# Linear attention, gated MLP and SoLU MLP on one core: where the small side products of a block and of the last layer stand in the engines' queues

## The chip, the cores and the metric

One NeuronCore of a Trainium2 chip. The metric is the device time of one execution in microseconds (us), as the median of several runs.

## The reference, cut to what matters

Eight batches of 576 tokens with 8 heads of 64 give 4,608 tokens of width 512.

```
q_s = softmax(q, over d);  k_s = softmax(k, over the sequence)
x   = q_s @ (k_s^T @ v)                      # per batch and head
y   = (silu(x @ w_gate) * (x @ w_val)) @ w_out            # d_ff 1536
h   = y @ w_in                                            # 512 -> 1024
s   = h * softmax(h);  out = (layernorm(s) * g_ln) @ w_out2
```

## The kernel before, in words

All matrix products are fp32 in three passes: each operand is split into a high part in fp32r and a low part (the rest), and `mm3` (L931 to L933) adds high x high, high x low and low x high. One pass is a matmul of 128x128 by 128x512.

The first layer runs in nine blocks of 512 tokens. A block has 12 slices of d_ff, and a slice takes three steps on PE, which the code calls gaps: `wg` (gate), the output product `y` of the slice two before it, and `wv` (value). So a block has 36 gaps of 12 matmuls. `block` sorts a table of tasks by gap; tasks of the same gap are recorded after the block's own step. The order of recording is the order in each engine's queue, and nothing reorders it later. `tasks_of(j)` puts the side work of block j there: the attention of the next tokens (gap 5: POOL's subtraction L540; gap 8: `q_max`, a DVE reduction and then POOL's subtraction L682; gap 9: `kv_exp`, the exp L601 on ACT; gap 11: `kv_mm`, the small product `pk` on PE, L610, that reads this exp; gap 14: `q_norm`, which ends in POOL's product L700; gaps 20, 24 and 26 the second half of k and v in the same way), and `y_forms_at`.

`y_forms_at` prepares y of the block before for the second layer. The product h = y w_in is done by seven products of halves instead of eight (Strassen's way in Winograd's form), for which y is needed in seven forms: three are quarters of y, four are sums and differences of them. `Y_FORMS` lists them in the order in which they are made: 0 to 2 plain, 3 to 6 with a sum. A form takes a sum on DVE (L895, only for forms 3 to 6), a cast on ACT (L913), the low part on DVE (L915), and two stores to DRAM (L917).

The second layer runs over 18 pairs of 128-token tiles. `emit_pair(p)` is the seven products (42 matmuls, named by their form: 1, 6, 5, 2, 7, 3, 4) with the additions that make h of them: `c` (ACT, L1342) copies the first product away before product 2 is accumulated on its bank. `emit_rest(p)` is the softmax, SoLU and the layer norm's sums of both tiles, their 16-bit halves `w`, the DMA transposes that turn them (`wT`), and the output products `emit_out` (48 matmuls) of the pair before. The turned halves are joined (`zt`, L1429 on DVE and L1432 on ACT) and split (`zhl`, L1440 on ACT, L1443 on DVE) inside the next pair's `emit_pair`. Its queue on ACT is, in this order: store, split of the first tile, `c`, join and split of the second tile.

The last block's y has no later block to make its forms in. Its last two output products run before pair 0's products and after them, `y_keep` copies y out of PSUM, and `y_make` makes the forms of pairs 16 and 17 in SBUF, seven in a row, in `emit_rest(14)` and `emit_rest(15)`. For the other pairs `y_load` brings the forms from DRAM.

Of the kernel before, what the change touches and what calls it, by code (L numbers as in the profile page):

```python
# [9 lines left out]
F32 = mybir.dt.float32  # L10
F32R = mybir.dt.float32r
# [5 lines left out]
PSUM = bass.MemoryType.PSUM  # L17
DRAM = bass.MemoryType.DRAM

P = 128  # L20
# [23 lines left out]
    banks=3,  # L44
# [161 lines left out]
def attention_glu_solu_kernel(  # L206
# [23 lines left out]
    nc = tc.nc  # L230
# [16 lines left out]
    NB = len(BLOCKS)  # L247
# [5 lines left out]
    def f32(ap):  # L253
        return ap.bitcast(F32)
# [21 lines left out]
    yf_dram = dram.tile([NT2 // 2, P, 2, 7, 2 * P], F32, name="yf_dram")  # L276
# [518 lines left out]
    tmp = ph1.enter_context(tc.tile_pool(name="tmp", bufs=1, reuse_waits="tile"))  # L795
# [8 lines left out]
    def at(t, g, f, *a):  # L804
        t.setdefault(g, []).append((f, a))
# [54 lines left out]
    ADD, SUB = ALU.add, ALU.subtract  # L860
    KH = KD // 2
    yts, yz = {}, {}

    def y_keep(j):


        if j < NB - 1:
            yt = tmp.tile([P, KD, Y2], F32, tag="yt", bufs=1, name="yt")
            halves_ = [yt[:, r * KH:(r + 1) * KH] for r in range(2)]
        else:  # L870
            halves_ = [apool.tile([P, KH, Y2], F32, tag="a", bufs=2, name="yt") for r in range(2)]
        for k in range(KD):
            o = halves_[k // KH][:, k % KH]
            if k % 2:
                nc.scalar.copy(out=o, in_=ys[j][k])
            else:
                nc.vector.tensor_copy(out=o, in_=ys[j][k])
        del ys[j]
        yts[j] = halves_

    def y_quarter(j, n, r):

        v = yts[j][r].rearrange("p k (q n t) -> p n q k t", q=2, n=2)
        return v[:, n]
# [34 lines left out]
    def y_forms_at(t, j):  # L919


        tasks = [Task(y_form, (j, n)) for n in range(7)]
        for n, g in enumerate((5, 6, 7, 8, 10, 12, 14)):
            at(t, g, tasks[n].step)
            at(t, g + 1, tasks[n].finish)

# [57 lines left out]
    def next_o(lag):  # L984
        if len(pend) > lag:
            emit_o(*pend.pop(0))
# [107 lines left out]
    psA = ExitStack()  # L1094
    w_b = wb.enter_context(tc.tile_pool(name="wb", bufs=1, reuse_waits="tile"))
    gv_pool = psA.enter_context(tc.tile_pool(name="ps_gv", bufs=4, space=PSUM))
# [130 lines left out]
    NP2 = NT2 // 2  # L1227
    FH = DF2 // 2
# [39 lines left out]

    yq = {}

    def q_tiles(p):
        homes = ((att, "qt"), (w_b, "b6")) if p % 2 else ((att, "kt"), (att, "vt"))
        yq[p] = [pool.tile([P, 7, KH, P], F32R, tag=tag, name=n) for (pool, tag), n in zip(homes, ("yh", "yl"))]

    def y_load(p):
        q_tiles(p)
        for n in range(2):
            nc.sync.dma_start(
                out=f32(yq[p][n]).rearrange("p i k t -> p (i k t)"),
                in_=yf_dram[p, :, n].rearrange("p i w -> p (i w)"),  # L1280
            )

    def y_make(p, n):

        j, q = divmod(p, 2)
        if n == 0:
            q_tiles(p)
        i, x, with_ = Y_FORMS[n]
        of = lambda n, r: y_quarter(j, n, r)[:, q]
        if with_:  # L1290
            if x and with_[0]:
                yz[j] = stat.tile([P, KH, P], F32, tag="m", bufs=1, name="yz")
            y_sum(yz[j], of, x, with_)
            s = yz[j]
        else:
            s = of(*x)
        yh, yl = (y[:, i] for y in yq[p])
        nc.scalar.copy(out=yh, in_=s)
        nc.vector.tensor_tensor(out=yl, in0=s, in1=f32(yh), op=SUB)

    t = tasks_of(NB - 1)
    at(t, 0, x_load)
# [9 lines left out]
    for p in range(2):  # L1312
        at(t, 28, y_load, p)
    block(NB - 1, range(NF), t)
    next_o(1)
    psA.close()
    l2s = ExitStack()
    ps_h = l2s.enter_context(tc.tile_pool(name="ps_h", bufs=1, space=PSUM, reuse_waits="tile"))

    ctx.enter_context(tc.manual_schedule())  # L1320

# [4 lines left out]
    banks, hhs, part = {}, {}, {}  # L1326

    def product(p, i):

        s, f, b, start = PRODUCTS[i]  # L1330
        if start:
            banks[b] = ps_h.tile([P, FH], F32, tag=f"h{b}", name=f"h{b}")
        yh, yl = yq[p]
        for kk in range(KH):
            mm3(
                banks[b], yh[:, s, kk], yl[:, s, kk], F[f][:, 0, kk], F[f][:, 1, kk],
                start and kk == 0, kk == KH - 1, start,
            )
# [17 lines left out]
    def h_other(p, n, uw, b):  # L1356
        nc.vector.tensor_tensor(out=hhs[p][:, n], in0=part["u"][:, uw], in1=banks[b], op=ADD)
# [3 lines left out]
    def h_of(t):  # L1361
        return hhs[t // 2][:, t % 2 * 2:t % 2 * 2 + 2]

    def emit_max(t):
        nm = stat.tile([P, 1], F32, tag="nm", bufs=3, name="nm")
        nc.vector.tensor_reduce(out=nm, in_=h_of(t), axis=AX.XY, op=ALU.max, negate=True)
        zs[t] = nm
# [23 lines left out]
    def emit_square(t):  # L1391
        junk = tmp.tile([P, DF2], BF16, tag="st", bufs=3, name="junk")
        svs[t] = sv = stat.tile([P, 1], F32, tag="sv", bufs=3, name="sv")
        nc.scalar.activation(out=junk, in_=zs[t], func=AF.Square, accum_out=sv)
# [33 lines left out]
    def emit_join_low(t):  # L1428
        nc.vector.tensor_copy(out=halves(zt_of(t))[0], in_=wTs[t][:, 0])  # L1429

    def emit_join_high(t):
        nc.scalar.copy(out=halves(zt_of(t))[1], in_=wTs.pop(t)[:, 1])  # L1432
# [5 lines left out]
    def emit_parts(t, lo):  # L1438
        if not lo:
            nc.scalar.copy(out=z_parts(t)[:, 0].rearrange("p c t -> p (c t)"), in_=zt_of(t))  # L1440
        else:
            zh, zl = (zT[t][:, n].rearrange("p c t -> p (c t)") for n in range(2))
            nc.vector.tensor_tensor(out=zl, in0=zt_of(t), in1=f32(zh), op=SUB)  # L1443
# [19 lines left out]
    def emit_out(t, cs=range(KF2), cols=1):  # L1463
        zh, zl = (zT[t][:, n] for n in range(2))
        n = DM // cols
        for i in range(cols):
            s = slice(i * n, (i + 1) * n)
            po = outs[t, i] = outs.get((t, i)) or y_bank(2 + (t + i) % 2)
            for c in cs:
                wh, wl = weight(("out", c))  # L1470
                first, last = c == 0, c == KF2 - 1
                nc.tensor.matmul(out=po[:, s], lhsT=zh[:, c, :], rhs=wh[:, s], start=first, stop=False)  # L1472
                nc.tensor.matmul(out=po[:, s], lhsT=zh[:, c, :], rhs=wl[:, s], start=False, stop=False)  # L1473
                nc.tensor.matmul(out=po[:, s], lhsT=zl[:, c, :], rhs=wh[:, s], start=False, stop=last)  # L1474
            if cols > 1:
                emit_store(t, i, s)
# [18 lines left out]
    last = NP2 - 1  # L1495

    def emit_pair(p):

        a, b = 2 * p - 2, 2 * p - 1
        back = p > 0
        product(p, 1)
        if p > 1:
            emit_store(a - 1)
        if back:
            emit_parts(a, 0)
        h_first(p)
        product(p, 6)
        if back:  # L1510
            emit_join_low(b)
            emit_join_high(b)
        h_u(p)
        product(p, 5)
        if back:
            emit_parts(a, 1)
            emit_parts(b, 0)
        h_w(p)
        product(p, 2)
        h_11(p)  # L1520
        if back:
            emit_parts(b, 1)
            emit_square(a)
            emit_square(b)
        product(p, 7)
        h_other(p, 3, 1, 3)
        product(p, 3)
        h_other(p, 1, 1, 1)
        product(p, 4)
        emit_max(2 * p)  # L1530
        h_other(p, 2, 0, 3)
        if back:
            emit_rstd(a)
            emit_rstd(b)

    def emit_rest(p, made):
        a, b = 2 * p, 2 * p + 1
        emit_e(a)
        emit_max(b)
        if 2 <= p + 2 < NP2 - 2:  # L1540
            y_load(p + 2)
        emit_e(b)
        if p == 0:
            next_o(0)
            y_keep_parts = y_keep(NB - 1)
        else:
            emit_out(a - 2)
        emit_solu(a)
        if p < last:
            emit_low(a)  # L1550
            emit_high(a)
        if p:
            emit_store(a - 2)
        for n in made:
            y_make(*n)
        emit_solu(b)
        if p < last:
            emit_low(b)
            emit_high(b)
            emit_join_low(a)  # L1560
            emit_join_high(a)
            if p:
                emit_out(b - 2)

    for p in range(last):
        emit_pair(p)
        emit_rest(p, [(p + 2, n) for n in range(7)] if NP2 - 2 <= p + 2 < NP2 else ())
    emit_pair(last)
    emit_rest(last, ())
    a, b = 2 * last, 2 * last + 1  # L1570
    emit_out(b - 2, range(4))
    emit_t(a)
# [7 lines left out]
    emit_out(a)  # L1580
    emit_store(a)
    emit_out(b, cols=2)
    l2s.close()
    wb.close()
    ph1.close()

# [27 lines left out]
```

## Time and profile before

| | |
|---|---|
| median of 3 runs (lowest to highest) | 1449.11 us (1448.65 to 1450.45) |
| the profiled execution's own time | 1453.04 us |
| its span, first to last instruction | 1451.3 us |
| mean granted TensorE clock | 0.967 of full speed |
| PE busy | 1367.9 us, 94% of the span |
| DVE, ACT, POOL busy | 59%, 48%, 9% |

The blocks run from the start to about 1046 us, the pairs from there to the end. PE is the engine to watch. A matmul counts as busy while it is in the pipeline, so short waits hide in its 94%; they show in the distance between the starts of two matmuls.

### The profile page before, as it was taken

Reading aid. Unit: us, or ns where it says so; the run is one execution under the profiler, and the core shown is the slowest. Engines: PE = TensorE matmul, PEld = TensorE weight load, DVE = VectorE, ACT = ScalarE, POOL = GpSimd, SP = SyncE. Lnnn points to the kernel's source line nnn. Section 1 sums busy time; section 2 is a strip of 40 time slices with the busy share of each in tenths; the row PEclk is TensorE's granted clock in tenths of the full one; section 3 lists DMA queues with packets and bytes.
Section 4 is the critical chain, followed back from the end, with each engine's and each line's share of the span. In section 5 each row is a group of like instructions: output and inputs, shape, how many; then the busy total and the mean of one; then the engine's idle time right before and its main releaser. Section 6 shows DMA issues by size and latency. Waiting matters only on the chain.

```text
span 1451.3 us, 17669 instructions
## 1 busy us (share of the span) xinstructions
PE 1367.9 (94%) x6705; PEld 1127.0 (78%) x6705; DVE 856.5 (59%) x1407; ACT 692.1 (48%) x963; POOL 134.5 (9%) x106
## 2 busy tenths in 40 slices
PE   6779989989989989999998999999979999999888
PEld 5558878878878868877887888888868888888667
DVE  6868656365355455455546526446177777777764
ACT  5765443334434424425425524333156666666554
POOL 3000022022022021021111002000000000000000
PEclk8889999999999999999999999999989999999999
DMA  9972756646746646557556556356355566556131
GB/s 281 285 257 91 207 162 161 151 151 171 178 145 163 167 171 163 150 157 186 141 160 192 174 174 189 141 189 223 115 144 160 153 189 170 163 142 185 44 73 43
DMA packets 276357, 238.15 MB, mean 164 GB/s; under 512 B 210352, under 2 KB 253360, under 8 KB 265520
## 3 DMA queue, kind: packets, MB, share of 16 engines
q1 hardware_dynamic: 276272, 237.02, 58.0%
q8 instruction: 53, 0.87, 0.2%
q14 instruction: 32, 0.26, 0.1%
HBM read 158.34 MB, written 53.48 MB: 146 GB/s over the span
## 4 chain that ended last, share of the span: by engine, by line
PE 77%; DVE 10%; DMA 5%; ACT 4%; issue 2%; SPq 1%; POOL 0%; DVEq 0%; ACTq 0%
PE wg L931 6%; PE wg L932 6%; PE wg L933 6%; PE y L931 6%; PE y L932 6%; PE y L933 6%; PE wv L931 6%; PE wv L932 6%; PE wv L933 6%; PE y L1473 3%; PE y L1474 3%; PE y L1472 3%; PE h L931 3%; PE h L932 3%; PE h L933 3%
## 5 line engine op out<-in xcount | busy, mean ns | idle before, releaser
L968 DVE TENSOR_TENSOR st<-st,wv 128x512 f32<-128x512 f32 x108 | 74.1, 686 | 238.5 <-PE wv L933 235.4
L972 ACT CAST a<-st 128x512 fp32r<-128x512 f32 x108 | 66.9, 619 | 259.7 <-DVE st L968 259.6
L931 PE MATMUL wg<-xh,wgv 128*128 128x512 f32 x432 | 176.2, 408 | 11.2 <-ACT wgv L335 10.5
L932 PE MATMUL wg<-xl,wgv 128*128 128x512 f32 x432 | 173.3, 401 | 0.3 <-DVE xl L784 0.3
L933 PE MATMUL wg<-xh,wgv 128*128 128x512 f32 x432 | 172.7, 400 | 0.0
L931 PE MATMUL y<-a,wo 128*128 128x512 f32 x432 | 169.1, 392 | 2.5 <-ACT a L972 2.5
L932 PE MATMUL y<-a,wo 128*128 128x512 f32 x432 | 169.2, 392 | 1.8 <-DVE a L974 1.8
L933 PE MATMUL y<-a,wo 128*128 128x512 f32 x432 | 169.1, 391 | 0.0
L931 PE MATMUL wv<-xh,wgv 128*128 128x512 f32 x432 | 168.5, 390 | 0.0
L932 PE MATMUL wv<-xl,wgv 128*128 128x512 f32 x432 | 168.1, 389 | 0.0
L933 PE MATMUL wv<-xh,wgv 128*128 128x512 f32 x432 | 168.1, 389 | 0.0
L974 DVE TENSOR_TENSOR a<-st,a 128x512 fp32r<-128x512 f32 x108 | 74.7, 691 | 76.5 <-ACT a L972 76.3
L1472 PE MATMUL y<-w,zhl 128*128 128x512 f32 (+1 forms) x296 | 113.7, 384 | 0.0
L1474 PE MATMUL y<-w,zhl 128*128 128x512 f32 (+1 forms) x296 | 113.5, 383 | 0.0
L1473 PE MATMUL y<-w,zhl 128*128 128x512 f32 (+1 forms) x296 | 113.5, 383 | 0.0
L931 PEld LDWEIGHTS wg<-xh,wgv 128*128 128x128 f32 x432 | 84.3, 195 | 30.3 <-ACT wgv L335 11.3
L963 ACT ACTIVATE st<-wg 128x512 f32<-128x512 f32 x108 | 64.5, 597 | 89.3 <-PE wg L933 89.0
L933 PEld LDWEIGHTS wg<-xh,wgv 128*128 128x128 f32 x432 | 84.1, 195 | 19.2 <-DVE wgv L345 1.1
L932 PEld LDWEIGHTS wg<-xl,wgv 128*128 128x128 f32 x432 | 84.7, 196 | 17.4 <-DVE xl L784 0.6
L931 PEld LDWEIGHTS y<-a,wo 128*128 128x128 f32 x432 | 81.5, 189 | 19.7 <-ACT a L972 2.9
L932 PEld LDWEIGHTS y<-a,wo 128*128 128x128 f32 x432 | 81.6, 189 | 18.8 <-DVE a L974 2.2
L933 PEld LDWEIGHTS y<-a,wo 128*128 128x128 f32 x432 | 81.7, 189 | 17.1
(264 smaller groups left out, 2552.8 us busy)
## 6 DMA issues: line engine op xcount, KB each, us to landing
wgv<-w_dram SPq DMA_DIRECT2D x64, 1024.0 KB, 5.3
yf_dram<-yf SPq DMA_DIRECT2D x112, 256.0 KB, 2.7
yh<-yf_dram SPq DMA_DIRECT2D x16, 896.0 KB, 4.8
yl<-yf_dram SPq DMA_DIRECT2D x16, 896.0 KB, 6.6
vt<-in_v_dram SPq DMA_DIRECT2D x64, 144.0 KB, 4.4
out_dram<-ot SPq DMA_DIRECT2D x35, 256.0 KB, 3.1
w_dram<-wgv SPq DMA_DIRECT2D x8, 1024.0 KB, 8.4
kt<-in_k_dram SPq DMA_DIRECT2D x56, 144.0 KB, 5.9
```

Source lines behind the costliest of these rows:

```text
L931: nc.tensor.matmul(out=po, lhsT=wh, rhs=rh, start=start, stop=False, **k)
L932: nc.tensor.matmul(out=po, lhsT=wh, rhs=rl, start=False, stop=False, **k)
L933: nc.tensor.matmul(out=po, lhsT=wl, rhs=rh, start=False, stop=stop, **k)
L963: nc.scalar.activation(out=st, in_=pg, func=AF.Silu)
L968: nc.vector.tensor_tensor(out=st, in0=st, in1=pv, op=ALU.mult)
L972: nc.scalar.copy(out=ah, in_=st)
L974: nc.vector.tensor_tensor(out=al, in0=st, in1=f32(ah), op=ALU.subtract)
L1472: nc.tensor.matmul(out=po[:, s], lhsT=zh[:, c, :], rhs=wh[:, s], start=first, stop=False)
L1473: nc.tensor.matmul(out=po[:, s], lhsT=zh[:, c, :], rhs=wl[:, s], start=False, stop=False)
L1474: nc.tensor.matmul(out=po[:, s], lhsT=zl[:, c, :], rhs=wh[:, s], start=False, stop=last)
```

## The change

It has three parts. First, forms 2 to 6 of y move to other gaps of a block. Second, both last output products stand behind pair 0's seven products, `y_keep` behind pair 0's SoLU, and the join and split of pair 0's tiles behind pair 1's product 7; the banks of the seven products come from the pool of `wg` and `wv`, which gives its four banks in turn, so that product 3 takes product 1's bank. Third, `y_make` makes one form per pair in pairs 1 to 14, on DVE and ACT as before, and stores it to DRAM; pairs 16 and 17 load their forms as the others do.

```diff
-        for n, g in enumerate((5, 6, 7, 8, 10, 12, 14)):
+        for n, g in enumerate((5, 6, 12, 13, 14, 15, 16)):
             at(t, g, tasks[n].step)
             at(t, g + 1, tasks[n].finish)
...
-        yh, yl = (y[:, i] for y in yq[p])
-        nc.scalar.copy(out=yh, in_=s)
-        nc.vector.tensor_tensor(out=yl, in0=s, in1=f32(yh), op=SUB)
+        f = tmp.tile([P, 2, KH, P], F32R, tag="st", bufs=3, name="yf")
+        nc.scalar.copy(out=f[:, 0], in_=s)
+        nc.vector.tensor_tensor(out=f[:, 1], in0=s, in1=f32(f[:, 0]), op=SUB)
+        nc.sync.dma_start(out=yf_dram[p, :, :, i], in_=f32(f).rearrange("p n k t -> p n (k t)"))
...
     block(NB - 1, range(NF), t)
-    next_o(1)
-    psA.close()
-    l2s = ExitStack()
-    ps_h = l2s.enter_context(tc.tile_pool(name="ps_h", bufs=1, space=PSUM, reuse_waits="tile"))
...
-            banks[b] = ps_h.tile([P, FH], F32, tag=f"h{b}", name=f"h{b}")
+            banks[b] = gv_pool.tile([P, FH], F32, tag="gv", name="h")
...
-        back = p > 0
+        back = p > 1
...
         product(p, 7)
+        if p == 1:
+            emit_join_low(a)
+            emit_join_high(a)
+            emit_parts(a, 0)
         h_other(p, 3, 1, 3)
+        if p == 1:
+            emit_parts(a, 1)
+            emit_join_low(b)
+            emit_join_high(b)
+            emit_parts(b, 0)
         product(p, 3)
...
         if p == 0:
+            next_o(1)
             next_o(0)
-            y_keep_parts = y_keep(NB - 1)
...
-        for n in made:
-            y_make(*n)
         emit_solu(b)
         if p < last:
             emit_low(b)
             emit_high(b)
-            emit_join_low(a)
-            emit_join_high(a)
             if p:
+                if p <= 14:
+                    y_make(NP2 - 2 + (p - 1) // 7, (p - 1) % 7)
+                emit_join_low(a)
+                emit_join_high(a)
                 emit_out(b - 2)
+            else:
+                y_keep(NB - 1)
```

What this does to the queues shows at three places. On ACT, in a block from gap 7 to gap 10 (`yf` is a form, `yt` y, `yz` its sum, `a` the gated slice, `st` its fp32 copy; - before, + now):

```order
-L913 CAST yf<-yt 128x512 x2
-L972 CAST a<-st 128x512
-L913 CAST yf<-yz 128x512
-L963 ACTIVATE st<-wg 128x512
-L601 ACT_TABLE_LOAD
-L601 ACTIVATE kt<-kt 96x1536
-L913 CAST yf<-yz 128x512
+L913 CAST yf<-yt 128x512
+L972 CAST a<-st 128x512
+L963 ACTIVATE st<-wg 128x512
+L601 ACT_TABLE_LOAD
+L601 ACTIVATE kt<-kt 96x1536
```

No form stands between the cast of `a` and the exp of `kt` any more. On DVE, in the same block from the end of `q_norm` at gap 14 on, before:

```order
L697 RECIPROCAL qs<-qs 128x32
L895 TENSOR_TENSOR yz<-yt 128x512
L915 TENSOR_TENSOR yf<-yz,yf 128x512
L968 TENSOR_TENSOR st<-st,wv 128x512
L974 TENSOR_TENSOR a<-st,a 128x512
```

And now:

```order
L697 RECIPROCAL qs<-qs 128x32
L915 TENSOR_TENSOR yf<-yz,yf 128x512
L895 TENSOR_TENSOR yz<-yz,yt 128x512
L915 TENSOR_TENSOR yf<-yz,yf 128x512
L895 TENSOR_TENSOR yz<-yt,yz 128x512
L915 TENSOR_TENSOR yf<-yz,yf 128x512
L895 TENSOR_TENSOR yz<-yt 128x512
L968 TENSOR_TENSOR st<-st,wv 128x512
L974 TENSOR_TENSOR a<-st,a 128x512
```

Between `q_norm` and the gated slice of gap 17 (L968, L974) there were two instructions of the forms, and there are six. On ACT, from pair 0's first copy `c` to pair 1's last split, before:

```order
L1342 COPY c_7794<-h_7787 128x512
L1354 COPY hh<-h_7787 128x512
L1373 ACT_TABLE_LOAD
L1373 ACTIVATE e,se<-hh,nm 128x1024 x2
L875 COPY yt<-y_7240 128x512
L875 COPY yt<-y_7242 128x512
L1419 COPY w<-e 128x1024 x2
L1432 COPY zt<-wT 128x1024
L1440 CAST zhl<-zt 128x1024
L1342 COPY c_7910<-h_7901 128x512
L1432 COPY zt<-wT 128x1024
L1440 CAST zhl<-zt 128x1024
```

And now (the lines are those of the changed kernel):

```order
L1335 COPY c_7778<-h 128x512
L1347 COPY hh<-h 128x512
L1366 ACT_TABLE_LOAD
L1366 ACTIVATE e,se<-hh,nm 128x1024 x2
L1412 COPY w<-e 128x1024 x2
L875 COPY yt<-y_7240 128x512
L875 COPY yt<-y_7242 128x512
L1335 COPY c_7901<-h 128x512
L1347 COPY hh<-h 128x512
L1425 COPY zt<-wT 128x1024
L1433 CAST zhl<-zt 128x1024
L1425 COPY zt<-wT 128x1024
```

Pair 1's `c` stood behind a join and a split of pair 0, and stands behind `y_keep` alone.

## Rows read from the trace of the kernel before

**Rows 1.** PE's waits over the span (engine, line, what for: us in total, times, longest).

```profile
PE pk L610 <- ACT kt L601: 30.6, 6, 5.4
...
PE h L931 <- ACT c L1342: 18.2, 3, 7.9
```

**Rows 2.** Windows of block 2: length, busy PE, PEld, DVE, ACT, POOL, PEclk, DMA share, GB/s.

```profile
319.00:321.00 2.00, 2.00 (x42) 2.00 (x42) 0.93 (x3) 0.90 (x3) 0.00 (x0) 0.50 0.00 0
...
323.00:325.00 2.00, 2.00 (x6) 1.56 (x6) 1.92 (x4) 1.24 (x1) 0.00 (x0) 0.54 0.04 8
```

**Rows 3.** Timeline of POOL, DVE and ACT in block 2 (start us, us, what).

```profile
310.06 3.86 POOL L682 TENSOR_TENSOR qt<-qt,qm 128x2048 f32<-128x2048 f32 x1 [3.75 <-DVE qm L680]
...
310.36 4.12 DVE L895 TENSOR_TENSOR yz<-yt 128x512 f32<-128x512 f32 x1
...
314.55 0.62 ACT L913 CAST yf<-yz 128x512 fp32r<-128x512 f32 x1 [7.63 <-DVE yz L895]
```

**Rows 4.** One line of the kernel, L968: durations ns min/median/max.

```profile
L968 DVE TENSOR_TENSOR st<-st,wv x108: 669/687/689, 56.7 to 1043.7; 128x512 f32<-128x512 f32 x108
```

**Rows 5.** Timeline of POOL, ACT, DVE and PE later in block 2.

```profile
336.45 3.88 POOL L700 TENSOR_TENSOR qt<-qt,qs 128x2048 f32<-128x2048 f32 x1 [14.80 <-DVE qs L697]
...
337.57 1.28 ACT L963 ACT_TABLE_LOAD   x1
...
337.58 3.30 DVE L915 TENSOR_TENSOR yf<-yz,yf 128x512 fp32r<-128x512 f32 x1 [0.73 <-ACT yf L913]
...
340.37 1.23 ACT L312 ACTIVATE w2r1r<-w2r1r,floor_bias 128x1024 uint32<-128x1024 uint8 x1
...
342.17 0.69 DVE L974 TENSOR_TENSOR a<-st,a 128x512 fp32r<-128x512 f32 x1 [0.69 <-ACT a L972]
...
350.28 0.39 PE L931 MATMUL y<-a,wo 128*128 128x512 f32 x1
```

**Rows 6.** Timeline of PE at the two ends of four pairs' products.

```profile
1058.41 0.39 PE L931 MATMUL h<-f,yh 128*128 128x512 f32 x1
...
1078.57 0.39 PE L1472 MATMUL y<-w,zhl 128*128 128x512 f32 x1
...
1171.63 0.39 PE L931 MATMUL h<-f,yh 128*128 128x512 f32 x1
...
1181.17 0.39 PE L1472 MATMUL y<-w,zhl 128*128 128x512 f32 x1
...
1356.61 0.39 PE L931 MATMUL h<-f,yh 128*128 128x512 f32 x1
...
1373.77 0.40 PE L1472 MATMUL y<-w,zhl 128*128 128x512 f32 x1
...
1384.67 0.39 PE L931 MATMUL h<-f,yh 128*128 128x512 f32 x1
...
1402.31 0.39 PE L1472 MATMUL y<-w,zhl 128*128 128x512 f32 x1
```

**Rows 7.** Timeline of DVE and ACT between pairs 0 and 1.

```profile
1058.31 1.28 DVE L877 COPY yt<-y 128x512 f32<-128x512 f32 x2
...
1059.58 1.05 ACT L875 COPY yt<-y 128x512 f32<-128x512 f32 x2
...
1065.49 1.04 ACT L1419 COPY w<-e 128x1024 uint16<-128x1024 uint16 x1 [2.25 <-DVE e L1388]
...
1069.91 0.58 ACT L1342 COPY c<-h 128x512 f32<-128x512 f32 x1
```

**Rows 8.** Timeline of ACT in a quiet pair, pair 6.

```profile
1171.45 1.36 ACT L1432 COPY zt<-wT 128x1024 uint16<-128x1024 uint16 x1 [1.08 <-DMA wT<-w]
...
1174.18 0.59 ACT L1342 COPY c<-h 128x512 f32<-128x512 f32 x1
```

**Rows 9.** One line of the kernel, L1298: durations ns min/median/max.

```profile
L1298 ACT CAST yh<-yz x8: 405/407/408, 1354.4 to 1386.1; 128x256 fp32r<-128x256 f32 x8
```

**Rows 10.** The page's DMA issues (times, KB each, us to landing).

```profile
yf_dram<-yf SPq DMA_DIRECT2D x112, 256.0 KB, 2.7
```

More of the change, by code (lines that the diff above doesn't have):

```diff
@@ L1269, in attention_glu_solu_kernel, with y_load @@
     yq = {}
-    def q_tiles(p):
+    def y_load(p):
         homes = ((att, "qt"), (w_b, "b6")) if p % 2 else ((att, "kt"), (att, "vt"))
         yq[p] = [pool.tile([P, 7, KH, P], F32R, tag=tag, name=n) for (pool, tag), n in zip(homes, ("yh", "yl"))]
-    def y_load(p):
-        q_tiles(p)
         for n in range(2):
@@ L1285, in y_make @@
         j, q = divmod(p, 2)
-        if n == 0:
-            q_tiles(p)
         i, x, with_ = Y_FORMS[n]
@@ L1501, in emit_pair @@
         a, b = 2 * p - 2, 2 * p - 1
-        back = p > 0
+        back = p > 1
         product(p, 1)
-        if p > 1:
+        if back:
             emit_store(a - 1)
-        if back:
             emit_parts(a, 0)
@@ L1529, in emit_pair, with emit_rest @@
         product(p, 4)
+        if p == 1:
+            emit_parts(b, 1)
         emit_max(2 * p)
         h_other(p, 2, 0, 3)
-        if back:
+        if p == 1:
+            emit_square(a)
+            emit_square(b)
+        if p:
             emit_rstd(a)
             emit_rstd(b)
-    def emit_rest(p, made):
+    def emit_rest(p):
         a, b = 2 * p, 2 * p + 1
@@ L1539, in emit_rest @@
         emit_max(b)
-        if 2 <= p + 2 < NP2 - 2:
+        if 2 <= p + 2 < NP2:
             y_load(p + 2)
@@ L1559, in emit_rest @@
             emit_high(b)
-            emit_join_low(a)
-            emit_join_high(a)
             if p:
+                if p <= 14:
+                    y_make(NP2 - 2 + (p - 1) // 7, (p - 1) % 7)
+                emit_join_low(a)
+                emit_join_high(a)
                 emit_out(b - 2)
+            else:
+                y_keep(NB - 1)
     for p in range(last):
         emit_pair(p)
-        emit_rest(p, [(p + 2, n) for n in range(7)] if NP2 - 2 <= p + 2 < NP2 else ())
+        emit_rest(p)
     emit_pair(last)
-    emit_rest(last, ())
+    emit_rest(last)
     a, b = 2 * last, 2 * last + 1
@@ L1582, in attention_glu_solu_kernel @@
     emit_out(b, cols=2)
-    l2s.close()
+    psA.close()
     wb.close()
```

## The prediction

> **What bounds the kernel now.** I read the page's busy shares first: PE is busy 94% of the span, so the question is where it stands still or runs slowly. The list of PE's waits answers that: nearly all of it behind the prologue is two entries [rows 1]. Six times, 5.1 us each, `pk` waits for the exp of `kt`; three times, 18.2 us together, a product of h waits for ACT's copy `c`. The windows around the first kind show a second loss: after the wait PE is granted 0.50 to 0.54 of its clock in three windows of 2 us, which is the lower of its two levels (1.2 of 2.4 GHz) nearly throughout [rows 2]. That takes 1.0 + 1.0 + 0.92 = 2.9 us more. So each of the six blocks with this wait loses 8.0 us, 48 us in all.
>
> Why the exp is late is in the timeline [rows 3]. POOL's L682 runs from 310.06 to 313.92. The sum L895 of form 3 starts on DVE at 310.36 and takes 4.12 us, until 0.56 us after POOL has ended. ACT's cast of that form waits 7.63 us, and behind the cast in the same queue stand the silu, the table load and the exp. The exp itself needs nothing from the form. So the long sum is not work: DVE was held while POOL read and wrote SBUF.
>
> For the pairs I compare the distance from the first product to the first output product. In a quiet pair it is 1181.17 - 1171.63 = 9.54 us for 42 matmuls, 0.227 each, and PE does not wait. Pair 1 takes 20.16, pair 15 17.16, pair 16 17.64 [rows 6]. Those three lose 10.6, 7.6 and 8.1 us, their slow clock included.
>
> **Part one, forms in other gaps.** Nothing is added or removed; 5 of 7 forms move behind `kv_mm`. No form stands ahead of the exp any more. Silu, table load and exp together take at most 3.8 us: today the cast ahead of them ends at 315.17 [rows 3], and PE is at work again in the window from 319.0 on [rows 2]. Behind the product that the silu reads, PE still has 24 matmuls to do before `pk`, 5.4 us at 0.227, so the exp is ready first. The next DVE instruction behind `q_max` is now L968, whose second operand lies in PSUM. In 108 executions it never took more than 0.689 us [rows 4], whatever POOL did beside it, so nothing is held at gap 8. Gain: 48 us if no new wait comes. The Trainium skill ("GPSIMD Engine Reference", Key points) says that POOL shares its SBUF interfaces with DVE and contends with DVE instructions that have two SBUF inputs or run in a two-port mode. By that rule L968 (one input in PSUM) is free, and L895, L915 and L974 are held wherever POOL works; the long L895 and L915 of the rows agree. Taken by itself the rule speaks against this change: it leaves both of POOL's long instructions where they are, and only lets them meet other forms, so that by it the sum could be as small as the 20 us of the other two parts. The rows decide how much of that reaches PE.
>
> One does, I think. L700 runs beside gap 14's forms already today: L915 was held for 3.30 us [rows 5], and nobody was hurt, since `a` of gap 17 was complete at 342.86 and its output product began at 350.28, a slack of 7.4. Now the held instruction is L895 of form 4, and behind it on DVE stand the rest of forms 4 to 6. Counted from POOL's end: 0.55 for the rest of the sum, as L915's today (340.88 against 340.33), 0.6 for ACT's cast [rows 3], then on ACT the table load, the silu and the two conversions, which took 4.03 (337.57 to 341.60) [rows 5], 0.6 for the cast of form 5, and 0.7 each, as L974, for L915 and the next sum. That is 7.2 before L968 of gap 17 gets DVE, where today it got it 0.5 after POOL's end; and `q_norm`'s reduction itself comes 1.3 later, behind forms 2 and 3. 7.2 - 0.5 + 1.3 = 8.0 against 7.4 of slack: a wait of 0.6 us on PE. The second half's exp, behind the same queues, may add half as much. I take 1.0 per block, 6 us. Bounds: nothing (if any of these overlap better) and 8.0 each (if the clock falls again and all is given back). The value is near the lower end, since what PE waits for comes 8.0 later where 7.4 are to spare.
>
> Blocks: 48 - 6 = 42 us. SP's loads of k and v and of a weight now stand ahead of the stores of forms 2 to 6 instead of behind them. What reads the forms is the second layer, after the last block, so a late store delays only the next form's buffer; that is in the bounds above.
>
> **Part two, pair 0 and pair 1.** PE's total is the same. Pair 0's products begin 12 matmuls earlier (2.7 us), so its SoLU ends earlier by that and by `y_keep`'s 1.28 on DVE: its last `w` is copied at about 1062.5 instead of 1066.53 [rows 7]. Then come `y_keep`'s two copies, 1.05, and `c`, 0.58: 1064.2. Product 2 of pair 1 is due at 1058.41 + 18 x 0.227 = 1062.5, so PE waits 1.7 us there. Today `c` ends at 1070.49, and PE waits 8.0. But pair 1's DVE queue now has the joins and low parts of pair 0 between its own sums and its maxima: four instructions over 128x1024, at L877's 0.64 per 512 columns some 5 us, part of it in waits. I expect pair 1's SoLU 3.5 us later against PE than in a quiet pair. A quiet pair's `c` ends at 1174.77 [rows 8] with product 2 due at 1171.63 + 18 x 0.227 = 1175.72, 0.95 of slack. So pair 2 waits about 2.7, and again a little at product 4, which stands behind the same DVE queue: 3.5 in all. Bounds: 0 and the 10.6 of pair 1 today. Gain: 10.6 - 1.7 - 3.5 = 5.4 us. Product 3's bank is now free after ACT's copy of product 2, which a quiet pair makes 0.6 us before it is wanted: nothing.
>
> **Part three, a form per pair.** Pairs 15 and 16 lose their 7.6 and 8.1 us, because SoLU of the second tile no longer stands behind seven forms. In pairs 1 to 14, ACT gets one cast of 0.41 [rows 9] and DVE two instructions of about the same; they stand where ACT waits 1.08 us for the transpose anyway [rows 8]. The cover is thin: with a sum ahead of it the cast ends some 0.4 us before the transpose lands. If it failed, each pair would pay at most 1.3 us (the chain of three) less 0.95 of slack. The store of 256 KB is issued behind both transposes of its pair, and lands in about 2.7 us [rows 10]. I take 1 us for all 14 pairs together; bounds 0 and 5. Gain: 15.7 - 1 = 14.7 us.
>
> **Sum.** 42 + 5.4 + 14.7 = 62 us. The profiled execution took 1453.04, so its like would take 1391; its own time is 3.9 above the median of the runs, and I take 62 from the median: 1387 us.
>
> **Rivals.**
> - *The held sum only changes place* (0.14). The order behind `q_norm` speaks for it, and the slack of 7.4 is used up by my own count. It decides where the wait for `a` passes some 4 us a block, since then the lower clock comes with it: 6 x 5 more lost, and 1417 us. (The skill's page named above would put it higher than I do.)
> - *The stores hold the transposes* (0.09). If each store kept the transposes for its whole 2.7 us, less 0.95 of slack, 14 pairs would pay 25 us: 1412. Against it: the store is behind them in the same queue. This is also the case that can end on the other side: from 62 / 14 = 4.4 us a pair on (5.4 us a store, twice its landing) it eats the whole gain, and at 6 us a pair the time is 1449 + 22 = 1471 (0.02 of the 0.09).
> - *The exp stays late* (0.05). If something other than the form held it, part one does nothing: 1449 - 20 = 1429. Against it: the exp's start follows the released cast without a pause.
> - *Everything hides* (0.06). No wait at gap 22, none in pair 2: 1387 - 6 - 5 = 1376.
> - My forecast, 1379 to 1396: 0.66.
>
> **The numbers.** The likeliest time is 1387. The range of 1376 to 1404 holds the forecast, the case in which all hides and a part of the first two rivals; what it leaves out is below 2 in 10. The bounds taken one by one say the same: all costs at nothing give 1376, and pair 2 at its upper bound with the stores at theirs gives 1398. A difference of less than 0.2% (2.9 us) can't be told from no change here. Faster needs only that more than 3 of the 62 us remain: 0.96; same 0.02; slower 0.02.
>
> **What would show it.** Part one: `pk` waits no more, the clock in blocks 1 to 6 is 1.00 throughout, and L895 takes 4 us at gap 14 instead of gap 8. A wait of output products for `a` (L972, L974) of 0.5 to 1 us per block would show the new limit. Part two: pair 1 from first to output product about 11.5 us, pair 2 about 13. Part three: pairs 15 and 16 at 9.5 to 10, and no pair between 3 and 14 above 10.2. I am wrong if the clock falls at the new short waits, or if transposes land later behind their `w` in pairs 1 to 14 than today.

## The result, and the profile after

| | before | after |
|---|---|---|
| median (lowest to highest), us | 1449.78 (1448.65 to 1453.89), 4 runs | 1398.36 (1397.22 to 1399.87), 4 runs |
| profiled execution, its span, us | 1453.04, 1451.3 | 1398.28, 1396.4 |
| mean granted TensorE clock | 0.967 | 0.987 |

The ratio is 0.9641, with a 95% interval of 0.9620 to 0.9662: 51.4 us gained between the medians, where 62 were predicted. Between the two profiled spans it is 54.9 us, since the profiled execution of before lies 3.3 us above its median; no row shows where.

The list of PE's waits of the kernel after (engine, line, what for: us in total, times, longest), against [rows 1]:

```profile
PE y L931 <- ACT a L972: 4.2, 7, 1.6
PE h L931 <- ACT c L1335: 4.0, 2, 2.5
...
PE y L932 <- DVE a L974: 3.2, 7, 1.8
PE px L777 <- ACT qhl L756: 3.1, 2, 1.5
```

The 30.6 us of `pk` are gone. What is left in the blocks is two kinds of short waits: output products for `a` (one of the seven, the longest, is in the first block and was there before), and twice the attention product `px` for the split queries `qhl` that it multiplies, a wait that the prediction does not name. The 18.2 us for `c` have become 4.0, in pairs 1 and 2.

Windows of block 2 after, at the place of [rows 2] (length, then busy time of PE, PEld, DVE, ACT, POOL, then the granted clock, DMA share, GB/s):

```profile
306.00:308.00 2.00, 2.00 (x51) 1.62 (x49) 0.69 (x1) 0.60 (x1) 0.56 (x1) 1.00 0.18 45
308.00:310.00 2.00, 2.00 (x13) 1.61 (x9) 1.16 (x4) 0.63 (x3) 0.14 (x1) 1.00 0.96 365
```

The clock is at its upper level throughout. The timeline of the same block after, POOL, DVE, ACT and PE around gaps 14 to 22 (start us, us, what; in brackets the idle time before and its releaser), answers to [rows 3, 5]:

```profile
323.53 3.88 POOL L700 TENSOR_TENSOR qt<-qt,qs 128x2048 f32<-128x2048 f32 x1 [15.13 <-DVE qs L697]
...
323.96 3.99 DVE L895 TENSOR_TENSOR yz<-yz,yt 128x512 f32<-128x512 f32 x1
...
328.03 0.62 ACT L913 CAST yf<-yz 128x512 fp32r<-128x512 f32 x1 [8.18 <-DVE yz L895]
...
331.45 1.23 ACT L312 ACTIVATE w2r1r<-w2r1r,floor_bias 128x1024 uint32<-128x1024 uint8 x1
...
335.27 0.62 ACT L972 CAST a<-st 128x512 fp32r<-128x512 f32 x1
...
335.92 0.69 DVE L974 TENSOR_TENSOR a<-st,a 128x512 fp32r<-128x512 f32 x1 [0.69 <-ACT a L972]
...
335.94 0.49 PE L931 MATMUL y<-a,wo 128*128 128x512 f32 x1 [0.39 <-ACT a L972]
...
336.66 0.50 PE L932 MATMUL y<-a,wo 128*128 128x512 f32 x1 [0.23 <-DVE a L974]
```

This is the chain that the prediction wrote out. The sum is held for as long as POOL works (323.96 to 327.95 against POOL's end at 327.41), ACT stands idle for 8.18 us before the cast, and behind the cast table load, silu and conversions have to be made up. The cast of `a` ends at 335.89, and the output product starts at 335.94: nothing is to spare. From the distances between the starts of PE's matmuls, less the usual 0.227 us, this costs 1.15 to 1.19 us in five of the six blocks and 1.43 in the first, 7.3 in all.

Block 5 after, around its gaps 23 to 27 (timeline of POOL, DVE, ACT, PE):

```profile
662.89 3.49 POOL L540 TENSOR_TENSOR kt<-kt,mt 96x1536 f32<-96x1536 f32 x1 [17.64 <-DVE mt L534]
...
664.07 2.87 DVE L974 TENSOR_TENSOR a<-st,a 128x512 fp32r<-128x512 f32 x1 [0.69 <-ACT a L972]
...
669.37 1.34 ACT L339 ACTIVATE w2r<-t,g_sb 128x512 fp32r<-128x512 f32 x2 [1.46 <-DVE t L324]
...
678.97 0.62 ACT L756 CAST qhl<-z 128x512 fp32r<-128x512 f32 x1
...
679.64 0.44 PE L777 MATMUL px<-qhl,kvh 128*128 128x384 f32 x1 [1.53 <-ACT qhl L756]
```

and its windows (columns as above):

```profile
680.00:682.00 2.00, 1.72 (x9) 1.45 (x9) 0.97 (x3) 1.39 (x2) 0.00 (x0) 0.79 1.34 228
682.00:684.00 2.00, 2.00 (x6) 1.61 (x5) 1.28 (x3) 0.76 (x2) 0.00 (x0) 0.50 1.37 197
```

The same place in the kernel before:

```profile
690.40 3.50 POOL L540 TENSOR_TENSOR kt<-kt,mt 96x1536 f32<-96x1536 f32 x1 [12.13 <-DVE mt L534]
...
693.94 0.69 DVE L968 TENSOR_TENSOR st<-st,wv 128x512 f32<-128x512 f32 x1 [3.61 <-PE wv L933]
```

POOL's subtraction for the second half of k (L540) waits for DVE's `mt` (L534). Before, it was over at 693.90, and the gated slice came behind it, since DVE had to wait 3.61 us for PE. After, the moved forms have made DVE late: L968 follows `mt` without a pause, and L974 begins 1.18 us into L540 and takes 2.87 us. In the kernel before no L974 took more than 0.694. Behind L974 on DVE stands the conversion of w_out2 (L320, L324), for which ACT's high part of it (L339) waits 1.46 us; behind that on ACT stand the scaling of `pk`, a table load, the silu and the split of q, whose cast `qhl` ends at 679.59. PE waits for it. In blocks 5 and 6 this takes 3.97 and 2.36 us by the distances of the starts, 6.3 together, the fallen clock of block 5 included. The earlier blocks lose 0.3 at most there: L974 is held in all six, but L339 runs only from block 5 on.

The pairs, timeline of PE (first product and first output product of pairs 1, 2 and 16), against [rows 6]:

```profile
1024.29 0.39 PE L931 MATMUL h<-f,yh 128*128 128x512 f32 x1
...
1035.60 0.39 PE L1465 MATMUL y<-w,zhl 128*128 128x512 f32 x1
...
1046.52 0.39 PE L931 MATMUL h<-f,yh 128*128 128x512 f32 x1
...
1060.40 0.39 PE L1465 MATMUL y<-w,zhl 128*128 128x512 f32 x1
...
1338.84 0.39 PE L931 MATMUL h<-f,yh 128*128 128x512 f32 x1
...
1348.38 0.39 PE L1465 MATMUL y<-w,zhl 128*128 128x512 f32 x1
```

Pair 1 takes 11.31 us (20.16 before), pair 2 13.88, pair 16 9.54 (17.64). Pair 15 takes 9.55. The timeline of ACT in pairs 1 and 2 answers to [rows 7, 8]:

```profile
1028.40 1.06 ACT L875 COPY yt<-y 128x512 f32<-128x512 f32 x2
1029.36 0.60 ACT L1335 COPY c<-h 128x512 f32<-128x512 f32 x1
...
1049.93 1.34 ACT L1425 COPY zt<-wT 128x1024 uint16<-128x1024 uint16 x1 [0.73 <-DMA wT<-w]
...
1052.65 0.58 ACT L1335 COPY c<-h 128x512 f32<-128x512 f32 x1
```

In pair 1 `c` stands right behind `y_keep`'s copies. In pair 2 it ends 6.71 us after the pair's first product, where pair 6 of before took 3.14 [rows 6, 8].

From the first matmul of block 1 to that of block 7, PE needs 674.7 us before (170.16 to 844.89) and 640.9 after (169.89 to 810.77): 33.9 are gained in these six blocks. Block 7 takes 100.64 in both. From block 8 to the end 20.7 are gained, and ahead of block 1 0.3. Together these are the 54.9 between the spans.

### The profile page after: what moved, and what is told of

It is laid out like the page before. It is cut to its first block, busy times and chain, and to the rows that moved or that the text cites. A ratio compares the mean times of both kernels' runs of the same rounds, so it can differ in the third digit from the quotient of the medians.

```text
span 1396.4 us, 17693 instructions
## 1 busy us (share of the span) xinstructions
PE 1351.4 (97%) x6705; PEld 1108.3 (79%) x6705; DVE 849.9 (61%) x1407; ACT 692.2 (50%) x963; POOL 132.8 (10%) x106
## 5 line engine op out<-in xcount | busy, mean ns | idle before, releaser
L968 DVE TENSOR_TENSOR st<-st,wv 128x512 f32<-128x512 f32 x108 | 73.8, 683 | 208.7 <-PE wv L933 205.1
L931 PE MATMUL wg<-xh,wgv 128*128 128x512 f32 x432 | 172.4, 399 | 11.7 <-ACT wgv L335 11.1
L932 PE MATMUL wg<-xl,wgv 128*128 128x512 f32 x432 | 170.4, 395 | 0.9 <-DVE xl L784 0.9
L933 PE MATMUL wg<-xh,wgv 128*128 128x512 f32 x432 | 170.2, 394 | 0.0
L974 DVE TENSOR_TENSOR a<-st,a 128x512 fp32r<-128x512 f32 x108 | 87.7, 812 | 65.1 <-ACT a L972 65.0
L931 PEld LDWEIGHTS wg<-xh,wgv 128*128 128x128 f32 x432 | 82.1, 190 | 30.2 <-ACT wgv L335 11.8
L931 PEld LDWEIGHTS y<-a,wo 128*128 128x128 f32 x432 | 81.3, 188 | 23.6 <-ACT a L972 7.2
L932 PEld LDWEIGHTS y<-a,wo 128*128 128x128 f32 x432 | 81.4, 188 | 22.0 <-DVE a L974 5.4
L933 PEld LDWEIGHTS wg<-xh,wgv 128*128 128x128 f32 x432 | 82.2, 190 | 18.1 <-DVE wgv L345 0.8
L933 PEld LDWEIGHTS wv<-xh,wgv 128*128 128x128 f32 x432 | 81.2, 188 | 17.0
```

Source lines behind the costliest of these rows:

```text
L931: nc.tensor.matmul(out=po, lhsT=wh, rhs=rh, start=start, stop=False, **k)
L932: nc.tensor.matmul(out=po, lhsT=wh, rhs=rl, start=False, stop=False, **k)
L933: nc.tensor.matmul(out=po, lhsT=wl, rhs=rh, start=False, stop=stop, **k)
L968: nc.vector.tensor_tensor(out=st, in0=st, in1=pv, op=ALU.mult)
L974: nc.vector.tensor_tensor(out=al, in0=st, in1=f32(ah), op=ALU.subtract)
```

## The experiments

**The parts alone (e1, e2).** The first run is the kernel before with part one only, the second the kernel after without it:

```diff
# e1, in the kernel before
-        for n, g in enumerate((5, 6, 7, 8, 10, 12, 14)):
+        for n, g in enumerate((5, 6, 12, 13, 14, 15, 16)):
# e2, in the kernel after
-        for n, g in enumerate((5, 6, 12, 13, 14, 15, 16)):
+        for n, g in enumerate((5, 6, 7, 8, 10, 12, 14)):
```

Expected of part one alone:

> The kernel before with the first part alone: forms 2 to 6 at gaps 12 to 16. My theory from the two traces: the six waits for the exp of kt go (48 us with their slow clock), a wait of 1.2 us for the gated slice comes in each of the six blocks and one of 4.0 and 2.4 us at the attention's px product in blocks 5 and 6, so 34 us less than before, about 1416 us. Rival: the parts help each other (stores, weights and loads share one DMA queue), then the parts alone do not add up to the whole and this one is above 1420 us.

Expected of parts two and three alone:

> The changed kernel with the forms back at their old gaps, so the second and third part alone. Theory: pair 1 loses 1.8 instead of 10.6 us, pair 2 loses 4.4, pairs 15 and 16 nothing instead of 15.7: 21 us less than before, about 1429 us, and the six waits for the exp stay at 5.1 us each. Rival (parts do not add up): above 1434 us.

Measured: part one alone 1420.73 us (1416.96 to 1421.94), ratio 0.9798 (0.9781 to 0.9814); parts two and three alone 1429.20 (1428.36 to 1429.52), ratio 0.9852 (0.9838 to 0.9867), beside 1450.5 for before. That is 29.8 and 21.3 us; together 51.1, which is the whole within the noise. Part one alone missed the 1416 that was expected and lies just above the rival's 1420, but the rival's reason, that the parts help each other, would need a sum clearly below the whole. PE's waits with part one alone:

```profile
PE h L931 <- ACT c L1342: 18.8, 3, 7.9
...
PE px L777 <- ACT qhl L756: 3.0, 2, 1.5
```

and with parts two and three alone:

```profile
PE pk L610 <- ACT kt L601: 30.7, 6, 5.5
...
PE h L931 <- ACT c L1335: 4.0, 2, 2.5
```

So no effect of one half on the other shows, and the waits for `px` come with part one. The 29.8 has an uncertainty that one trace can't place: the profiled execution of e1 is its fastest (1416.96, 33.5 below before's median), the other three lie at 1420.7 to 1421.9.

**A held sum that starts later (e3).** Forms 4 to 6 each one gap later, so that ACT's table load and conversions stand ahead of form 4's cast and not behind it:

```diff
-        for n, g in enumerate((5, 6, 12, 13, 14, 15, 16)):
+        for n, g in enumerate((5, 6, 12, 13, 15, 16, 17)):
```

> The changed kernel with forms 4, 5 and 6 one gap later, at 15, 16 and 17. On DVE the sum of form 4 stays behind the end of the query normalisation and is held by GpSimd as before (4 us); on ACT the silu, the table load and the two conversions of gap 15 now stand ahead of form 4's cast, so they run while DVE is held. Theory (the new wait is the held sum plus the ACT work that stands behind it): the gated slice of gap 17 comes about 4 us earlier, the six waits of 1.2 us are gone and the two px waits shrink, together 8 to 13 us less than the changed kernel, 1386 to 1390 us. Rival (the hold alone makes the wait, whatever stands behind it on ACT): no difference, 1398 us.

Measured: 1386.66 us (1385.74 to 1387.09), ratio 0.9559 (0.9545 to 0.9574), 11.7 less than the kernel after, as the theory had it. Its timeline in block 2 (DVE and ACT):

```profile
322.22 1.23 ACT L312 ACTIVATE w2r1r<-w2r1r,floor_bias 128x1024 uint32<-128x1024 uint8 x1
...
323.51 3.99 DVE L895 TENSOR_TENSOR yz<-yz,yt 128x512 f32<-128x512 f32 x1
...
330.28 0.62 ACT L972 CAST a<-st 128x512 fp32r<-128x512 f32 x1
```

The sum is still held, for the same 3.99 us. But L312, which ran at 331.45 after it, is now over before it starts, and the cast of `a` comes 5.0 us earlier (0.5 of it because the whole timeline stands earlier). No output product waits for `a` in blocks 1 to 6 any more; from 200 to 900 us this is the whole list of PE's waits:

```profile
PE px L778 <- DVE qhl L757: 0.5, 2, 0.3
```

So at this place the hold costs through what stands behind it on ACT, not by its length alone. The waits for `px` shrink to 0.8 us a block: L974 of block 5 is held for 2.87 as before, but L339 now starts at 662.13, not 669.37, against 5.7 by which the whole timeline there stands earlier.

**The cause of the late exp before (e4).** The kernel before, with POOL's subtraction L682 left out for blocks 2 to 8 (q's maximum is not taken off there):

```diff
-        eng.tensor_tensor(
-            out=qt, in0=raw, in1=qm.to_broadcast([n, nc_, nh, D]), op=ALU.subtract
-        )
+        if j < 2:
+            eng.tensor_tensor(
+                out=qt, in0=raw, in1=qm.to_broadcast([n, nc_, nh, D]), op=ALU.subtract
+            )
```

> The kernel before without GpSimd's subtraction of the queries' maximum for blocks 2 to 8 (the softmax does not need it for these values; the maximum is still taken). Nothing else is moved: form 3 with its sum still stands ahead of the exp. Theory (the exp of kt was late because GpSimd held the sum): L895 takes 0.7 us at gap 8, the six waits for the exp go with their slow clock, 48 us less than before, 1402 us. Rival (the exp was late because three forms stood ahead of it on ScalarE, held or not): at least half of each wait stays, above 1420 us.

Measured: 1419.04 us (1416.73 to 1421.85), ratio 0.9788 (0.9760 to 0.9815). The 1402 were missed, and the waits are shorter than the half that the rival wanted: each theory had a part of it. PE's waits:

```profile
PE pk L610 <- ACT kt L601: 10.1, 6, 2.0
```

and its timeline in block 2 (DVE and ACT; lines below L682 are numbered one higher):

```profile
301.42 2.28 DVE L680 TENSOR_REDUCE qm<-qt 128x32 f32<-128x2048 f32 x1
...
304.22 0.68 DVE L896 TENSOR_TENSOR yz<-yt 128x512 f32<-128x512 f32 x1
...
304.98 0.62 ACT L914 CAST yf<-yz 128x512 fp32r<-128x512 f32 x1 [4.20 <-DVE yz L896]
```

The sum falls from 4.12 to 0.68, so POOL did hold it. The wait falls from 5.1 to 1.7 us each, and the loss per block from 8.0 to some 2.0, since the clock mostly stays up. What remains is not POOL: the form's sum stands behind the reduction of 2.28 us, and ACT still idles 4.20 us for it with the exp behind. So the hold was 3.4 of the 5.1 us and nearly all of the slow clock; the place of the form was the rest. Moving the form, as the change does, takes away both.

**The hold in the kernel after (e5).** L700 left out for blocks 2 to 8 (the queries are not normalised there; the edit is the same `if j < 2:` around L700):

> The changed kernel without GpSimd's product that normalises the queries (blocks 2 to 8 keep their queries unnormalised; the sums and reciprocals are still made). Theory (GpSimd holds DVE at gap 14, and the late DVE queue then makes the px waits of blocks 5 and 6): L895 takes 0.7 us everywhere, the waits for the gated slice (7.3 us in all) and the two px waits (6.3 us) both go: 1385 us. Rival (the px waits come from the weight conversion of gap 24, which only blocks from 5 on have, and not from the hold): only the 7.3 us go, 1391 us, and px still waits 4.0 and 2.4 us.

Measured: 1392.23 us (1391.08 to 1397.46), ratio 0.9606 (0.9584 to 0.9627). PE's waits from 200 to 900 us:

```profile
PE px L778 <- ACT qhl L757: 2.7, 2, 1.6
...
PE y L932 <- ACT a L973: 0.2, 1, 0.2
```

The waits for `a` are gone but for one of 1.01 us by the starts, so L700's hold makes them. The waits for `px` stay (1.91 and 3.94 us): as the rival had it, they don't come from L700. L540 is nearly as late as with L700 (69.7 us into block 5 against 71.3), and the held L974 (here L975) is still there:

```profile
656.40 3.50 POOL L540 TENSOR_TENSOR kt<-kt,mt 96x1536 f32<-96x1536 f32 x1 [35.09 <-DVE mt L534]
...
657.53 2.92 DVE L975 TENSOR_TENSOR a<-st,a 128x512 fp32r<-128x512 f32 x1 [0.69 <-ACT a L973]
```

**The conversion behind the split of q (e6).** The kernel after, with the high and low parts of w_out2 (L339 on ACT, L349 on DVE) at gap 28 in place of 24; the joins L320 and L324 stay at gap 23:

```diff
-        at(t, 24, parts_of_w2, j - 1)
+        at(t, 28, parts_of_w2, j - 1)
...
-        at(t, 24, store_w2, j - 1)
-        at(t, 25, stream_next, j, STREAM.index(None))
+        at(t, 28, store_w2, j - 1)
+        at(t, 29, stream_next, j, STREAM.index(None))
```

> The changed kernel with the high and low parts of w_out2 made at gap 28 instead of 24 (their store with them, the next load of a weight at 29 instead of 25). Theory after the run without the query product (the px waits of blocks 5 and 6 come from this conversion, which stands in the queues ahead of the query split when the DVE queue is late): px waits under 1 us in both blocks instead of 4.0 and 2.4, 1393 us; the six waits for the gated slice stay at 1.2. Rival (the low part held by GpSimd at gap 23 makes them late alone): px waits as before, 1398 us.

Measured: 1395.71 us (1393.19 to 1397.50), ratio 0.9619 (0.9595 to 0.9644), an interval that overlaps that of the kernel after. The time alone does not decide; PE's waits from 200 to 900 us do, where this list is the whole answer:

```profile
PE y L931 <- ACT a L972: 2.6, 6, 0.7
PE y L932 <- DVE a L974: 1.3, 6, 0.2
```

No `px` is left, and the waits for `a` stay. So the place of these parts is what turned DVE's lateness into a wait of PE. How much of the lateness is the held L974 no run shows, since none leaves L540 out; the hold is 2.18 us (2.87 - 0.69), about what block 6 loses (2.36). In this profiled execution the first block's wait for weights is 3.3 us longer than in the profile of after (14.4 against 11.1), which hides most of the gain in its own time.

**Part three undone (e7).** The kernel after, with the forms of pairs 16 and 17 made seven in a row again:

```diff
+        if NP2 - 2 <= p + 2 < NP2:
+            for n in range(7):
+                y_make(p + 2, n)
         emit_solu(b)
...
-                if p <= 14:
-                    y_make(NP2 - 2 + (p - 1) // 7, (p - 1) % 7)
```

> The changed kernel with the third part undone: pairs 16 and 17 get their seven forms in a row in SBUF, in pairs 14 and 15. Theory: pairs 15 and 16 lose 15.7 us again, 1413 to 1414 us, and pairs 1 to 14 stay as they are, pair 2 with its 4.4, since the one form per pair cost them nothing. Rival (the form and its store per pair cost the pairs something): pair 2 and the small waits of pairs 3 to 13 (1.8 us together) shrink, below 1411 us.

Measured: 1414.25 us (1413.37 to 1415.38), ratio 0.9749 (0.9727 to 0.9771), 15.9 above the kernel after. PE's waits:

```profile
PE h L931 <- ACT c L1338: 15.1, 5, 5.4
```

Pairs 15 and 16 lose 7.73 and 7.52 us again. Pairs 3 to 14 lose 2.6 together without any form in them, and 1.8 with one in each (the kernel after): a form per pair costs nothing that shows. Pair 2 loses 3.6 here and 4.35 there, the difference that the last section is about. No run has part two alone; this run less part one alone leaves 6.7 us for it (36.5 less 29.8), where 5.4 were predicted.

**Both repairs (e8).** The kernel after, with forms 4 to 6 one gap later and the conversion at gap 28:

> Forms 4 to 6 at gaps 15 to 17 and the parts of w_out2 at gap 28, on the changed kernel. Theory: with the first alone 1386.7 us and 0.5 us of px wait left in each of blocks 5 and 6, so 1 us less than that, 1385.7 us. Rival (the conversion at gap 28 now meets the query split of the later heads): 1387 us or more.

Measured: 1385.39 us (1382.91 to 1387.12), ratio 0.9548 (0.9524 to 0.9571). No `a` of blocks 1 to 6 and no `px` is waited for: PE's list from 200 to 900 us holds only one wait of 0.3 us for a weight. It beats both kernels, and can't be told from the run with the forms alone (1386.66): that run had only 1.7 us of `px` left to give.

## Why the prediction was right, and where it was too high

The range held, and the chosen case was the right one. The likeliest time was 11.4 us too low, and most of that lies in the blocks. A wait that the prediction had not seen fitted into the range only because the range was wide enough; that part is luck.

- *The exp no longer waits*: right. Six losses of 8.0 us are gone, with their slow clock. That a held sum caused them is shown by e4 for 3.4 of the 5.1 us; the prediction told of the hold alone, and the remaining 1.7 was the form's place behind the reduction. Nothing is held at gap 8 any more, as predicted, but the 108 executions of L968 were thinner evidence than they look: in only 6 of them did it run beside a POOL instruction (L540, at 0.69 us). In the kernel after no DVE instruction runs beside L682 at all.
- *The held sum moves to gap 14 and makes `a` late*: right in place and mechanism; e3 and e5 show the cause. The wait worked out for `a` was 0.6 us a block, and 1.15 to 1.43 came. The chain behind POOL's end was right (7.2 predicted, 334.55 - 327.41 = 7.1 measured); the term "`q_norm`'s reduction itself comes 1.3 later" was too small, since L700 starts 13.8 us ahead of the time at which the output product is due in the kernel before and 11.9 in the kernel after, 2.0 later. That the 1.0 chosen for the block, 6 in all, lies so near the 7.3 is partly luck: it held an addition for the second half. The clock did not fall there, so the rival in which the held sum only changes place did not come.
- *"The second half's exp, behind the same queues, may add half as much"*: this is the step that failed. PE never waited for that exp. But DVE's queue, late by the moved forms, met POOL's second subtraction, which held L974, and with the conversion of w_out2 behind L974 the split of q was late for `px` in blocks 5 and 6: 6.3 us that no term held. The blocks so gained 33.9 of the 42 in the profiled execution, and 29.8 between the medians of e1. Of the 8.1 missing in the profiled execution, 6.3 are these and 1.3 are `a` (7.3 against 6). The prediction followed the moved forms to the next output product and not through the rest of the block, and did not look at the two blocks in which the second half of k and the conversion meet.
- *Pairs 1 and 2*: pair 1 was put at about 11.5 and took 11.31; the wait for `c` was put at 1.7, and the pair lost 1.8. Pair 2 was put at about 13 and took 13.88; it lost 4.35 where 3.5 was the term, and 3.6 in e3, where the clock stayed up. The place was right too: ACT's `c` stands behind the join of a transpose that lands late.
- *A form per pair*: the 15.7 of pairs 15 and 16 came back whole, and the 1 us for the fourteen forms was not needed (e7). The bound of 10.2 for pairs 3 to 14 was passed once, by pair 10 with 10.39; that need not be the form, since without it (e7) pairs 9, 10 and 13 lose 1.17, 0.33 and 0.54. The rival of the stores is out.
- *The sum*: 62 predicted, 54.9 between the spans. The blocks give 8.1 less, the pairs 20.7 where 20.1 were due, the part ahead of block 1 gives 0.3 that no term held. Between the spans' 54.9 and the medians' 51.4 lies what single executions differ by. The prediction had seen that the profiled execution of before lay above its median, and still took the whole sum from the median.

The Trainium skill ("GPSIMD Engine Reference", Key points) names contention of POOL with DVE instructions that have two inputs in SBUF. The rows agree at three places: L895 3.99, L974 2.87, L915 3.30 [rows 5], and L968 with an input in PSUM never above 0.69 [rows 4]. At a fourth they don't show a hold of DVE. At gap 5 two L915, with both inputs in SBUF, run beside POOL's first subtraction in each of the blocks 1 to 6, before and after; in block 2 of the kernel after:

```profile
294.83 1.25 DVE L915 TENSOR_TENSOR yf<-yt,yf 128x512 fp32r<-128x512 f32 x2
...
295.04 4.40 POOL L540 TENSOR_TENSOR kt<-kt,mt 96x1536 f32<-96x1536 f32 x1 [49.18 <-DVE mt L534]
```

The second of them starts 0.36 us into L540 and takes 0.68, its usual time; here POOL's instruction is the long one, 4.40 against 3.49 for the second half of k. These runs don't explain which of the two engines is held when they meet, and the prediction's "held wherever POOL works" is too broad. And the 20 us that it drew from the rule taken by itself is not what came: e3 has the same holds, and they cost it no wait for `a` and some 1.7 us for `px`.

## What to carry to other kernels

In these runs a held instruction cost what stood behind it in the queues of the engines that waited for it: put work that needs nothing from it ahead of its consumer (one gap gave 11.7 us here), or keep the instruction away from POOL's long ones. When side work is moved, follow every later step of that round on each engine, above all long POOL instructions that now meet others, and rounds with an extra task of their own. Work that is in a hurry at the end, such as seven forms in a row, can be spread one by one over rounds in which the engine waits anyway; here that had no cost that shows.

## What was not expected of the hardware

The same wait of PE brought the lower clock in some executions and not in others. Pair 2's products in the kernel after, windows around the wait for `c`:

```profile
1050.00:1052.00 2.00, 0.76 (x4) 0.30 (x2) 0.69 (x1) 2.00 (x3) 0.00 (x0) 1.00 1.02 193
1052.00:1054.00 2.00, 0.71 (x2) 0.62 (x3) 0.66 (x2) 1.89 (x3) 0.00 (x0) 0.81 1.07 309
1054.00:1056.00 2.00, 2.00 (x6) 1.53 (x5) 2.00 (x4) 1.73 (x2) 0.00 (x0) 0.50 0.08 28
```

and in e3, around the same wait:

```profile
1040.00:1042.00 2.00, 0.24 (x1) 0.24 (x2) 0.16 (x1) 1.87 (x4) 0.00 (x0) 1.00 1.12 273
1042.00:1044.00 2.00, 2.00 (x10) 1.62 (x10) 2.00 (x3) 1.97 (x2) 0.00 (x0) 1.00 0.30 114
```

The waits are alike (2.5 us each in the lists), but the first is followed by 0.50, the lower level, and the second by 1.00. Of the experiments with these pairs, e6 and e8 have the fall; e2, e3, e5 and e7 have none. The wait for `px` in block 5 shows the same: 1.5 us for `qhl` in the kernel after and in e1, with a fall to 0.50 in the first and none in the second (2.29 us lost there, 3.97 in the kernel after). What decides it these runs don't show; a loss behind a wait of this size is uncertain by 0.7 to 1.7 us here (pair 2 and block 5).
